# Moving batch 1's values and mixing steps into batch 0's output product, and the second channel weight's transfers ahead of them

## The chip, the cores and the metric

The kernel runs on one core of one Trainium2 chip. The metric is device time in microseconds (us) of one execution, as the median of several. Lower is better. The text calls the engines by the profile's names: PE is the matrix engine, DVE, ACT and POOL are the vector, scalar and GpSimd engines, and SP only issues transfers.

## The reference, cut to what matters

For each of 8 batches there are 8 heads of masked attention over 576 positions, and then an MLP mixer that works first across tokens and then across channels.

```
scores = scale * q @ k.T             # (8 batches, 8 heads, 576, 576), head_dim 64
masks: heads 0-3 see the last 32 positions; heads 4-7 every 4th of the last 128
attn = softmax(where(mask, scores, -1e9)) ; x = attn @ v   # as (batch, 576, 512)
xt = x.transpose(0, 2, 1)
h = maximum(xt @ w_tok1, 0) @ w_tok2          # 576 -> 256 -> 576, over tokens
u = x + h.transpose(0, 2, 1)
h2 = maximum(u @ w_ch1, 0) @ w_ch2            # 512 -> 1536 -> 512, over channels
out = u + h2
```

Inputs and output are float32; the kernel computes in float16 with float32 accumulation.

## The kernel before, in words

The work is one fully unrolled program. Every engine runs its instructions in the order in which the program writes them. For each batch there are these stages, named here by the tiles that the profile prints:

- **Loads and casts.** SP issues the float32 loads of q, k and v (tiles `l_q`, `l_k`, `lt` for the tails, `l_vn`, `l_vt`, `l_vd`, `l_vx`). POOL casts them to float16 (`c_q`, `c_k`, `c_t`, `vv`, `vt`; all of them at L102). A cast of q or k covers two heads, so it comes four times for each, numbered 0 to 3.
- **Turning q and k over.** PE transposes a cast tile into a PSUM bank, and ACT or DVE copies it out (L309 to L340 for batch 1; `bare_steps`, L363 to L391, for batch 2: one step `tails`, and q and k steps 0 to 3).
- **Scores.** PE multiplies, ACT takes the exponential out of PSUM (batch 1: L453 to L496, one pair of heads at a time). From batch 2 on `scores_twin` (L498) does two pairs of heads in one group of 24 matmuls at L510, which write six PSUM banks, then eight or so exponentials at L534, then masks on POOL.
- **Values.** Eight heads; PE into a bank (`av`, L592 to L617), and DVE divides by the row's sum into `xn`.
- **Token mixing.** h1: four steps of five matmuls (L619), with the relu on ACT. u: five steps, s = 4, 0, 1, 2, 3 in this order (L630); for batch 1 the sum with `xn` is taken by PE and copied out by ACT for s = 0 and 2, and by DVE for s = 4, 1, 3. Then u is transposed, four steps `emit_uT` (L656), each of which reads all of s = 0 to 3.
- **Channel products.** The first, `gp` (L768): 12 blocks of four 512-column matmuls with the weight `w3`, each evacuated with a relu into `gt`. The second, the output product `yp` (L801): 4 row blocks of two halves, each half 12 matmuls of 256 columns, with the weight `w4`; its first six matmuls use blocks 0 to 7 of `w4` at most, the next six use blocks 6 to 11. DVE adds u, and SP stores.

PSUM has eight banks, under three tags: `main` (3, for `gp` and `yp`), `sc` (2, for scores) and `fl` (3, for nearly everything else: transposes, values, h1, u, uT). A step that needs a bank of `fl` waits until an earlier user's copy out of a bank is done. The twin score group of batch 2 takes **all three** `fl` banks at once (L500 to L503): the first two for the scores of heads 0 and 1, the third for the small blocks and tails.

**The order around the change.** `interleave` (L827) writes the order by a planner's clock t in rough us. The main stream of a batch (its `gp`, then its `yp`) yields planned costs of 0.43 for half a `gp` block and 0.65 for a piece (six matmuls, half of a half) of `yp`. Every other step is a tuple (due time, cost, function); when its due time is at or below t, the step is written next, and t grows by its cost. While batch 0's two products run, the steps of batch 1's scores, values, mixing and uT, and the first of batch 2's, are written among them. Batch 1's `gp` starts when batch 0's `yp` is written out, and it needs all of batch 1's uT.

**Transfers of the weights.** `w3` (three parts) and `w4` (three parts, L999) are issued on POOL, so each issue stands in POOL's order among the casts. In the kernel before, the third part of `w3` is issued after the first two casts of batch 1, and the three parts of `w4` after the first twelve of them. Behind batch 1's last cast stands a `gate` (L867, L1006): a cast of one element from the first part of `w4` into batch 2's tail tile. SP can issue batch 2's loads only when that is done.

Of the kernel before, what the change touches and what calls it, by code (L numbers as in the profile page):

```python
# [68 lines left out]
def kernel(  # L69
# [181 lines left out]
    def cast_qk(b, nm, hp, eng):  # L251
        if (b, nm) not in c16:
            c16[(b, nm)] = sb.tile([128, 4, 4, 2, D], FP16, tag=f"c_{nm}", bufs=1, name=f"c_{nm}_{b}")
        copy(eng, c16[(b, nm)][:, hp],
             l32[(b, nm, hp // 2)][:, 2 * (hp % 2):2 * (hp % 2) + 2].rearrange("m h r d -> m r h d"))

    def cast_tails_qk(b, eng):
        c16[(b, "t")] = sb.tile([128, H, D], FP16, tag="c_t", bufs=1, name=f"c_t_{b}")
        copy(eng, c16[(b, "t")], l32[(b, "t")])

    def cast_tail_v(b, eng):
        copy(eng, vv[b % 2][0:64, 4, :, 0:64], l32[(b, "vt")])

    def cast_vn(b, s, eng):
        copy(eng, vv[b % 2][:, s, 0:4, 0:64], l32[(b, "vn")][:, s])

    def cast_vd(b, h, eng):
        copy(eng, vv[b % 2][:, 0:4, 4 + h:6 + h, 0:64],
             l32[(b, "vd")][:, h:h + 2].rearrange("m h r d -> m r h d"))

    def cast_vx(b, eng):
        copy(eng, vt[b % 2][:, :, 0:64], l32[(b, "vx")])

    def cast_steps(b, eng=nc.gpsimd):
        steps = [lambda: cast_tails_qk(b, eng)]
        for hp in range(4):
            for nm in ("q", "k"):
                steps.append(lambda nm=nm, hp=hp: cast_qk(b, nm, hp, eng))
        for s in range(4):
            steps.append(lambda s=s: cast_vn(b, s, nc.gpsimd))  # L280
        steps.append(lambda: cast_tail_v(b, nc.gpsimd))
        for h in (0, 2):
            steps.append(lambda h=h: cast_vd(b, h, nc.gpsimd))
        steps.append(lambda: cast_vx(b, nc.gpsimd))
        return steps
# [59 lines left out]
    def twinned(b):  # L345
        return b >= 2
# [81 lines left out]
    def veiled(b, hp):  # L428
        return b <= 1
# [249 lines left out]
    def turned(b):  # L679
        return b >= 2  # L680
# [18 lines left out]
    def score_steps(b, t0, dt, offs=(0.0, 0.7, 2.0), places=None, lag=0.0):  # L699

        steps = []
        if twinned(b):
            for g in range(2):
                f = scores_twin(b, g)
                at = t0 + g * dt
                steps.append((at, 0.86, lambda f=f: next(f)))
                for i in range(7 if g else 9):
                    steps.append((at + lag * (i + 1), 0.0, lambda f=f: next(f)))
            return steps
        for hp in range(4):  # L710
            at, at_s = places[hp] if places else (t0 + hp * dt, t0 + hp * dt + dt)
            for nm in ("q", "k"):
                steps.append((at + 0.9 * (nm == "k"), 0.28, lambda nm=nm, hp=hp: transposes(b, nm, hp)))
            g = (scores_plain if hp < 2 else scores_dil)(b, hp)
            for i in range(3):
                steps.append((at_s + offs[i], 0.42 if veiled(b, hp) else 0.21, lambda g=g: next(g)))
        return steps

    def value_steps(b, t0, dt):
        steps = []  # L720
        for h in range(H):
            def step(h=h):
                if h == 0:
                    xn[b] = sb.tile([128, 5, DM], FP16, tag="xn", bufs=2, name=f"xn_{b}")
                values(b, h)
            steps.append((t0 + dt * h, 0.29 if h < 4 else 0.18, step))
        return steps

    def mix_steps(b, t_h1, t_h1b, t_u, t_uT, du=1.0, turn=6.0, gap=2.6):
        h1 = [sb.tile([128, DM], FP16, tag="h1", bufs=4, name=f"h1_{b}_{jb}") for jb in range(2)]  # L730
        steps = []
        for half, at in ((0, t_h1), (1, t_h1b)):
            for jb in range(2):
                steps.append((at + 0.9 * jb, 0.55, lambda jb=jb, half=half: emit_h1(b, jb, half, h1[jb])))
        for i, s in enumerate((4, 0, 1, 2, 3)):
            steps.append((t_u + du * i, 0.44, lambda s=s: emit_u(b, s, h1)))
        if turned(b):
            for t, tail in ((2.0, True), (turn, False))[1 - b % 2:]:
                steps.append((t_u + t * du, 0.0, lambda tail=tail: uT_dma(b, tail)))
            for t, cb in ((0.0, 2), (0.0, 0), (gap, 3), (gap, 1)):  # L740
                steps.append((t_uT + t, 0.0, lambda cb=cb: uT_place(b, cb)))
        else:
            for i, cb in enumerate(CBS):
                steps.append((t_uT + 0.9 * i, 0.28, lambda cb=cb: emit_uT(b, cb)))
        return steps
# [155 lines left out]
    va = [st[2] for st in value_steps(0, 0.0, 1.0)]  # L901
# [90 lines left out]
    casts1 = cast_steps(1)  # L992
    for i in (0, 1):
        casts1[i]()
    load_w3(2)
    for i in (2, 4, 5, 7, 6, 8, 9, 10, 11):
        casts1[i]()
    for i in range(3):
        nc.gpsimd.dma_start(  # L999
            out=w4a[:, 4 * i:4 * i + 4],  # L1000
            in_=moe_w_ch2[512 * i:512 * i + 512, :].rearrange("(p i) c -> p i c", i=4))
    for cast in casts1[12:]:
        cast()

    new_qk(2)
# [8 lines left out]
    def at(t0, dt, fs):  # L1014
        return [(t0 + dt * i, 0.0, f) for i, f in enumerate(fs)]

    for b in range(B):
        steps = []
        if b == 0:
            steps += at(2.9, 0.0, [lambda: cast_qk(1, "q", 1, nc.scalar)])  # L1020
            steps += score_steps(1, 0, 0, (0.0, 0.7, 1.5),
                                 ((3.0, 4.9), (4.3, 6.6), (6.9, 9.2), (8.3, 11.0)))
            va = value_steps(1, 13.2, 0.7)
            steps += va[:4] + [(p + 0.3, c, f) for p, c, f in va[4:]]
            steps += mix_steps(1, 18.4, 20.8, 22.8, 31.4, 1.1)
            steps += at(24.0, 0.3, cast_steps(2))
            bare = bare_steps(2)
            scores2 = score_steps(2, 29.6, 4.4, lag=0.25)
            scores2 = sorted(scores2, key=lambda st: st[0])
            steps += [(t, 0.25, f) for t, f in zip((25.4, 26.4, 27.2, 28.0, 28.8, 34.8, 35.2, 35.6, 36.0), bare)]  # L1030
            steps += scores2[:10]
            steps += at(34.0, 0.0, [lambda: emit_loads_qk(3)])
        elif b == 1:
            va = value_steps(2, 0.0, 1.0)
            steps += [(0.8 + 0.4 * i, c, f) for i, (_, c, f) in enumerate(scores2[10:])]
            steps += [(t, c, f) for t, (_, c, f) in zip((2.2, 3.0, 4.8, 5.6, 8.2, 9.0, 10.4, 11.2), va)]
            steps += mix_steps(2, 7.0, 13.0, 15.1, 24.6, 1.0, 5.6, 0.8)
            casts = cast_steps(3)
            steps += [(6.0 + 0.5 * i, 0.0, casts[i]) for i in (0, 2, 4, 6, 8)]
            steps += [(9.5 + 1.0 * i, 0.0, lambda i=i: cast_qk(3, "q", i, nc.scalar)) for i in range(4)]  # L1040
            steps += score_steps(3, 21.0, 4.6, lag=0.1)
            steps += at(20.8, 0.9, load_steps(4))
            loads, turns, places = [], dma_steps(3), place_steps(3)

            def some_v(lo, hi):
                if not loads:
                    loads.extend(load_v_steps(3))
                for f in loads[lo:hi]:
                    f()

            steps += at(6.0, 0.0, [lambda: some_v(0, 4)]) + at(8.1, 0.0, [turns[0], turns[2], lambda: some_v(4, 7)])
            steps += at(10.6, 0.0, [turns[1], turns[4], lambda: some_v(7, 8)]) + at(12.6, 0.0, [turns[3]])
            steps += at(11.0, 0.3, casts[9:14]) + at(12.5, 0.0, places[0:3])
            steps += at(13.0, 0.3, casts[14:16]) + at(14.0, 0.0, places[3:]) + at(14.2, 0.0, casts[16:])
        else:
            late = 2.4 * (b % 2)
            if b + 1 < B:
                steps += value_steps(b + 1, 0.4, 0.95) + mix_steps(b + 1, 5.4 + late / 6, 9.0, 11.4, 22.4 + late)
            if b + 2 < B:
                steps += at(2.0, 0.6, cast_steps(b + 2)) + score_steps(b + 2, 16.6 + 1.25 * late, 4.5)  # L1060
                steps += at(8.5, 0.7, dma_steps(b + 2)) + at(12.0, 0.4, place_steps(b + 2))
            if b + 3 < B:
                steps += at(17.6, 0.9, load_steps(b + 3))
        interleave(gen_main(b), steps)
# [30 lines left out]
```

## Time and profile before

| | us |
|---|---|
| median of 3 runs | 286.30 (285.88 to 286.33) |
| the profiled execution | 286.22 |
| its span, first to last instruction | 284.4 |
| PE busy | 276.2 (97%) |
| ACT, DVE, POOL busy | 136.9, 130.7, 163.3 |
| batch 0's `gp` starts | 26.74 |
| batch 0's first `yp` matmul | 48.53 |
| batch 1's `gp` starts | 67.47 |

The profiled execution's own time is 1.8 us longer than its span. In a row of the timeline the columns are the start in us, the duration in us, the engine, the line, the operation, the tiles written and read, the shapes, and in brackets how long the engine stood idle before it and what ended that. A matmul's row lasts longer than its turn on PE, because matmuls overlap: matmuls of 512, 256 and 128 columns follow each other after 0.215, 0.110 and 0.056 us, while their rows are 0.38, 0.27 and 0.22 us long.

### The profile page before, as it was taken

To read this page: it belongs to the slowest core of one execution; us is meant where nothing else is said; L and a number is where in the kernel's file an instruction comes from. 1 tells how busy PE (TensorE), PEld (TensorE's weight loads), DVE (VectorE), ACT (ScalarE), POOL (GpSimd) and SP (SyncE) were. 2 spreads that over 40 slices of the span, in tenths; PEclk is the share of its full clock that TensorE was granted. 3 is DMA by queue.
4 is the path that set the end of the run, shared out by engine and by line. 5 is a ranking of instruction groups with operands and counts; after the bars stand their busy time and mean duration, and the time that the engine had idled before them with its cause. 6 is when DMAs were issued, how large, how long until landed. Compare 5 with 4: busy or idle time off the path is not lost.

```text
span 284.4 us, 7021 instructions
## 1 busy us (share of the span) xinstructions
PE 276.2 (97%) x2850; PEld 210.9 (74%) x2850; DVE 130.7 (46%) x275; ACT 136.9 (48%) x270; POOL 163.3 (57%) x220
## 2 busy tenths in 40 slices
PE   6899999999999999999999999999999999999995
PEld 2786677887676976697776976797767966896595
DVE  7776676356764155415640254426441274421022
ACT  2863765454454615383446625482546534225500
POOL 7980760587936998459961999179953930000000
PEclk9999999999999999999999999999999999999999
DMA  7999999984999999999979988299974210431023
GB/s 218 265 227 253 271 218 211 323 206 117 342 187 142 292 275 236 145 223 334 195 151 227 312 239 169 58 236 313 203 146 85 94 56 2 92 112 39 0 76 111
DMA packets 105695, 52.63 MB, mean 185 GB/s; under 512 B 73888, under 2 KB 104608, under 8 KB 105664
## 3 DMA queue, kind: packets, MB, share of 16 engines
q1 hardware_dynamic: 101424, 47.07, 69.2%
q0 software_dynamic: 2640, 3.94, 7.9%
q10 hardware_dynamic: 1600, 1.18, 1.4%
q8 instruction: 22, 0.36, 0.6%
q14 instruction: 9, 0.07, 0.1%
HBM read 37.07 MB, written 9.44 MB: 163 GB/s over the span
## 4 chain that ended last, share of the span: by engine, by line
PE 79%; DMA 7%; POOL 6%; SPq 2%; DVE 2%; issue 1%; ACT 1%; POOLq 0%; ACTq 0%
PE gp L768 25%; PE yp L801 25%; PE h1p L627 4%; PE gt L759 4%; PE up L639 4%; PE yp L818 3%; PE sc L510 2%; DMA l_k<-in_k_dram 2%; DMA w1p<-in_moe_w_tok_dram 2%; DMA kr<-c_k 2%; DMA l_q<-in_q_dram 2%; POOL c_q L102 1%; PE av L603 1%; PE av L608 1%; PE h1p L625 1%
## 5 line engine op out<-in xcount | busy, mean ns | idle before, releaser
L801 PE MATMUL yp<-w,gt 128*128 128x256 f16 x744 | 85.8, 273 | 0.0
L801 PEld LDWEIGHTS <-gt 128*128 128x128 f16 x744 | 76.1, 106 | 6.4
L106 ACT ACTIVATE gt<-gp 128x512 f16<-128x512 f32 x71 | 42.4, 597 | 73.5 <-PE gp L768 73.2
L768 PE MATMUL gp<-utd,w 128*128 128x512 f16 x144 | 54.7, 380 | 0.0
L768 PE MATMUL gp<-utm,w 128*128 128x512 f16 x144 | 54.6, 379 | 0.0
L768 PEld LDWEIGHTS <-w 128*128 128x128 f16 x384 | 38.9, 114 | 19.7 <-issue 0.5
L809 DVE TENSOR_TENSOR o<-yp,u 128x512 f32<-128x512 f32 x31 | 21.4, 692 | 63.4 <-PE yp L801 63.4
L112 POOL TENSOR_TENSOR attp<-attp,const 128x1280 f16<-128x1280 f16 x12 | 31.4, 2616 | 24.4 <-ACT attp L534 24.3
L112 DVE TENSOR_TENSOR xn<-av,rec 128x320 f16<-128x320 f32 x64 | 31.5, 492 | 2.2
L112 POOL TENSOR_TENSOR attd<-attd,const 128x1024 f16<-128x1024 f16 x12 | 25.4, 2134 | 1.9 <-ACT attd L534 1.9
L768 PE MATMUL gp<-uT,w 128*128 128x512 f16 x96 | 25.8, 380 | 0.0
L108 DVE TENSOR_SCALAR gt<-gp 128x512 f16<-128x512 f32 x25 | 17.2, 688 | 13.7 <-PE gp L768 13.0
L645 DVE TENSOR_TENSOR u<-up,xn 128x512 f16<-128x512 f32 x26 | 17.9, 690 | 6.2 <-PE up L639 6.2
L534 ACT ACTIVATE attp<-sc 128x480 f16<-128x480 f32 (+1 forms) x36 | 16.1, 536 | 7.3 <-PE sc L510 6.2
L102 POOL CAST c_k<-l_k 128x512 f16<-128x512 f32 x29 | 17.7, 622 | 2.1 <-DMA l_k<-in_k_dram 2.0
L102 POOL CAST c_q<-l_q 128x512 f16<-128x512 f32 x26 | 16.7, 648 | 2.5 <-DMA l_q<-in_q_dram 1.8
L106 ACT ACTIVATE h<-h1p 128x256 f16<-128x256 f32 x31 | 11.9, 384 | 11.9 <-PE h1p L627 11.5
L616 DVE RECIPROCAL rec<-av 128x5 f32<-128x5 f32 x64 | 12.2, 191 | 9.8 <-PE av L613 9.6
L399 POOL COPY kt<-kr 128x512 f16<-128x512 f16 x10 | 10.8, 1078 | 9.9 <-DMA kr<-c_k 7.7
L697 ACT COPY utd<-utm 128x512 f16<-128x512 f16 x12 | 12.7, 1117 | 5.8 <-DMA utm<-u 5.8
L102 POOL CAST vv<-l_vn 128x256 f16<-128x256 f32 x32 | 11.9, 413 | 4.0 <-DMA l_vn<-in_v_dram 4.0
L112 POOL TENSOR_TENSOR attt<-attt,const 128x512 f16<-128x512 f16 x12 | 13.9, 1162 | 0.0
(149 smaller groups left out, 465.2 us busy)
## 6 DMA issues: line engine op xcount, KB each, us to landing
out_dram<-o SPq DMA_DIRECT2D x71, 128.0 KB, 3.2
l_q<-in_q_dram SPq DMA_DIRECT2D x15, 512.0 KB, 6.7
l_k<-in_k_dram SPq DMA_DIRECT2D x14, 512.0 KB, 7.1
l_vn<-in_v_dram SPq DMA_DIRECT2D x32, 128.0 KB, 6.4
l_vd<-in_v_dram SPq DMA_DIRECT2D x16, 256.0 KB, 4.5
w<-in_moe_w_ch_dram POOLq DMA_DIRECT2D x6, 512.0 KB, 7.6
lt<-in_q_dram SPq DMA_DIRECT2D x8, 128.0 KB, 3.9
l_vt<-in_v_dram SPq DMA_DIRECT2D x8, 128.0 KB, 4.1
```

The lines of the kernel that those rows point to most:

```text
L102: eng.tensor_copy(out=out, in_=in_)
L106: nc.scalar.activation(out=out, in_=in_, func=AF.Relu)
L108: eng.tensor_scalar_max(out=out, in0=in_, scalar1=0.0)
L112: eng.tensor_tensor(out=out, in0=x, in1=y, op=ALU.mult)
L534: nc.scalar.activation(out=out, in_=in_, func=AF.Exp, scale=0.125)
L616: nc.vector.reciprocal(out=rec[:, :, 0], in_=av[:, :, 64])
L627: nc.tensor.matmul(out=p, lhsT=w[:, s, j], rhs=x[:, s, c], start=False, stop=(s == 3))
L645: nc.vector.tensor_tensor(out=u16(b, s), in0=blocks4(p), in1=blocks4(xn[b][:, s]), op=ALU.add)
L697: nc.scalar.copy(out=natural(uTd[:, cb - 2]), in_=uTm[i][:, cb].rearrange("p r m -> p m r"))
L768: nc.tensor.matmul(out=p, lhsT=w3_block(cb, mb), rhs=uT[(b, cb)][0], start=(i == 0), stop=(i == 3))
L801: nc.tensor.matmul(out=p[:, c], lhsT=gta[:, mb, a0:m0 + 512:4] if half else gta[:, mb, a0:a0 + 128], rhs=w4[mb][:, c], start=(mb == 0), st ...
L809: nc.vector.tensor_tensor(out=blocks4(o32), in0=blocks4(p), in1=u16(b, s), op=ALU.add)
```

## The change

The three issues of `w4` move from behind batch 1's twelfth cast to places among its casts: one after the casts of k 0 and 1, one after q 2 and 3, one after k 2 and 3. In batch 0's plan, batch 1's scores are spread a little wider; the values move from due time 13.2 to 20.4, the four h1 steps from 18.4 and 20.8 to 25.4 and 27.4, the u steps from 22.8 with a spacing of 1.1 to 28.8 with 0.95, and uT from 31.4 to 33.6. Batch 2's first casts, transposes and first score group move by 1 to 2.4. In batch 1's plan the score groups of batch 3 move by 0.5.

```diff
     load_w3(2)
-    for i in (2, 4, 5, 7, 6, 8, 9, 10, 11):
-        casts1[i]()
     for i in range(3):
+        for c in ((2, 4), (5, 7), (6, 8))[i]:
+            casts1[c]()
         nc.gpsimd.dma_start(
             out=w4a[:, 4 * i:4 * i + 4],
             in_=moe_w_ch2[512 * i:512 * i + 512, :].rearrange("(p i) c -> p i c", i=4))
-    for cast in casts1[12:]:
+    for cast in casts1[9:]:
         cast()
...
             steps += score_steps(1, 0, 0, (0.0, 0.7, 1.5),
-                                 ((3.0, 4.9), (4.3, 6.6), (6.9, 9.2), (8.3, 11.0)))
-            va = value_steps(1, 13.2, 0.7)
+                                 ((3.0, 5.2), (4.6, 7.2), (7.4, 10.0), (9.4, 12.2)))
+            va = value_steps(1, 20.4, 0.65)
             steps += va[:4] + [(p + 0.3, c, f) for p, c, f in va[4:]]
-            steps += mix_steps(1, 18.4, 20.8, 22.8, 31.4, 1.1)
-            steps += at(24.0, 0.3, cast_steps(2))
+            steps += mix_steps(1, 25.4, 27.4, 28.8, 33.6, 0.95)
+            steps += at(25.6, 0.3, cast_steps(2))
             bare = bare_steps(2)
-            scores2 = score_steps(2, 29.6, 4.4, lag=0.25)
+            scores2 = score_steps(2, 32.0, 4.4, lag=0.25)
             scores2 = sorted(scores2, key=lambda st: st[0])
-            steps += [(t, 0.25, f) for t, f in zip((25.4, 26.4, 27.2, 28.0, 28.8, 34.8, 35.2, 35.6, 36.0), bare)]
+            steps += [(t, 0.25, f) for t, f in zip((26.6, 27.6, 28.6, 29.8, 30.6, 35.2, 35.7, 36.2, 36.7), bare)]
...
-            steps += score_steps(3, 21.0, 4.6, lag=0.1)
+            steps += score_steps(3, 21.5, 4.6, lag=0.1)
```

## The prediction

> **What bounds the kernel now.** I read the cores' row first, then the busy times, and then went only to PE.
>
> ```profile
> core 0: 284.4 us, clock 0.998
> ```
> ```profile
> PE 276.2 (97%) x2850; PEld 210.9 (74%) x2850; DVE 130.7 (46%) x275; ACT 136.9 (48%) x270; POOL 163.3 (57%) x220
> ```
>
> PE is the bound, at full clock. The change adds and removes no matmul, so only PE's waits can move the time, and a wait removed or added in batch 0's stage goes to the end one to one: nothing behind it is idle enough to give it back. Next come PE's waits from batch 0's `gp` (26 us) to batch 1's (67.4 us), and the two of them that the waits view is too coarse for.
>
> ```profile
> PE sc L425 <- DVE kt L314: 0.5, 2, 0.4
> PE sc L510 <- DVE kt L385: 0.5, 1, 0.5
> ```
> ```profile
> 38.98 0.19 PE L423 MATMUL sm<-veil,const 128*128 128x64 f16 x1
> 39.01 0.19 PE L425 MATMUL sm<-qz,kt 128*128 128x64 f16 x1
> 39.28 0.22 PE L423 MATMUL sc<-veil,const 128*128 128x128 f16 x1
> ```
> ```profile
> 59.42 1.50 PE L801 MATMUL yp<-w,gt 128*128 128x256 f16 x12
> 60.88 0.27 PE L673 MATMUL tpu<-const,u 128*128 128x128 f16 x2
> ```
>
> The middle rows show how to read an idle time: matmuls follow each other every 0.03 us but last 0.19, so each idle figure hides about 0.16 us more. Three waits then cost 0.5 + 0.32 = 0.82 (batch 1's scores for k's copy) and 0.5 + 0.16 = 0.66 (batch 2's score group for the same). The fourth is 39.01 to 39.28, 0.24 (a bank of `sc`). The fifth: twelve `yp` matmuls at 0.110 end at 60.74, and uT starts at 60.88, so 0.14. Together 1.86 us: all that better placing could gain here.
>
> **Scores and first product.** I wrote the planner's order out by hand from the due times and costs; for the kernel before it gives the sequence of the trace. In the new order one half of `gp` more stands between each k transpose and its score, but DVE's chain of copies in front is as long as before and `gp` block 5's relu joins it. I leave 0.28 of the 1.06 (0.82 + 0.24) there; bounds 0 and 1.06. Gone: 0.78. Batch 2's score group now stands behind u steps, its k copy is done earlier, and uT stands elsewhere: 0.66 + 0.14 gone. Total gone **1.58**.
>
> **When `yp` starts.** Ahead of the first `yp` the new order has eight values and two h1 steps fewer.
>
> ```profile
> 48.53 0.82 PE L801 MATMUL yp<-w,gt 128*128 128x256 f16 x6
> 49.18 0.27 PE L625 MATMUL h1p<-xn,w1t 128*128 128x256 f16 x1
> 49.29 0.60 PE L627 MATMUL h1p<-xn,w1p 128*128 128x256 f16 x4
> 49.73 0.27 PE L625 MATMUL h1p<-xn,w1t 128*128 128x256 f16 x1
> ```
>
> An h1 step is 0.55 (49.18 to 49.73), a piece of `yp` (six matmuls, half of a half) 0.65 (48.53 to 49.18); values at the planner's costs are 4 x 0.29 + 4 x 0.18 = 1.88. First `yp`: 48.53 - 1.88 - 1.10 - 0.78 = **44.8**; the third part of `w4` is needed after eight more matmuls, at 45.7.
>
> **The transfers.** The next rows are POOL's timeline; then the two queues' shares of the 16 DMA engines in three stretches, 32.5 to 35, 35 to 41 and 41 to 49 us (q0 is POOL's, q1 SP's); then the landing times of `w4`'s parts.
>
> ```profile
> 33.49 1.18 POOL L102 CAST c_k<-l_k 128x512 f16<-128x512 f32 x2 [0.35 <-DMA l_k<-in_k_dram]
> ...
> 38.08 1.62 POOL L999 DMA_DIRECT2D w<-in_moe_w_ch_dram  x3
> ...
> 41.71 0.41 POOL L102 CAST vt<-l_vx 128x256 f16<-128x256 f32 x1
> 43.67 0.18 POOL L867 CAST lt<-w 1x1 f32<-1x1 f16 x1 [1.55 <-DMA w<-in_moe_w_ch_dram]
> 50.88 0.62 POOL L102 CAST c_t<-lt 128x512 f16<-128x512 f32 x1 [7.03 <-DMA lt<-in_k_dram]
> 52.16 0.61 POOL L102 CAST c_q<-l_q 128x512 f16<-128x512 f32 x1 [0.67 <-DMA l_q<-in_q_dram]
> 53.67 0.62 POOL L102 CAST c_k<-l_k 128x512 f16<-128x512 f32 x1 [0.90 <-DMA l_k<-in_k_dram]
> ```
> ```profile
> q0 software_dynamic: 383, 0.39, 93.5%
> q1 hardware_dynamic: 447, 0.12, 29.3%
> ```
> ```profile
> q1 hardware_dynamic: 2419, 0.99, 71.9%
> q0 software_dynamic: 164, 0.31, 34.4%
> ```
> ```profile
> q0 software_dynamic: 380, 1.36, 86.1%
> ```
> ```profile
> DMA to landing us min/median/max: 5.5/7.4/10.4
> ```
>
> An issue costs POOL 1.62 / 3 = 0.54 us. The three of them now delay casts of q and k 2 and 3 by 0.54 and 1.08, which the wider scores cover, and the last is issued at about 35.8. The DMA engines are full from 32 on, so an earlier issue only changes who goes first. From 35 on, q0 (rest of `w3`, all of `w4`) needs 34.4% of 6 + 86.1% of 8 = 8.95 us, and q1 (batch 1's v) 71.9% of 6 = 4.3: together 13.3, at the 1.0 to 1.2 that full stretches reach done at 46 to 48.3; I take 47.3. In the first stretch the queues took turns packet by packet (383 to 447), so POOL's long packets took three quarters of the time. On that share `w4` runs ahead (8.95 / 0.93 from 35, 44.6; landing about 1 later, **45.6**, just in time for 45.7) and v ends last, its landing, final cast and the gate (0.2 + 0.41 + 0.18) at **48.1** instead of 43.85. Batch 2's loads start 4.3 later.
>
> [...] Service in order of issue instead would be the late-weight rival below.
>
> From the gate's end to the end of batch 2's tail cast took 51.50 - 43.85 = 7.65, to the first k cast 54.29 - 43.85 = 10.44, with `w4`'s end still in the way; I take 0.7 off each for that, an estimate: 55.1 and 57.8. On PE the values start five pieces after 44.8, at 48.1; batch 2's tails follow after the values, five more pieces and two h1 steps, 1.88 + 5 x 0.65 + 1.10, at 54.35, and wait 0.75; the first k transposes follow 2.2 later (0.22, 0.65, 0.55, 0.22, 0.55), at 57.3, and wait 0.5. Sum with 0.1 for `w4`: **1.35**, bounds 0 (gate at 46.5 or before) and 3 (gate at 48.6, nothing taken off).
>
> **The u chain.** What copies banks out, on ACT and then DVE (49 to 67 us), and the end of the small exponentials:
>
> ```profile
> L383 ACT COPY qt<-tp_q 128x512 f16<-128x512 f16 x4 | 2.4, 590 | 2.2 <-PE tp_q L378 2.2
> L643 ACT CAST u<-up 128x512 f16<-128x512 f32 x2 | 1.2, 588 | 2.0 <-PE up L639 2.0
> ```
> ```profile
> L102 DVE COPY uT<-tpu 128x640 f16<-128x640 f16 x3 | 1.8, 599 | 1.7 <-PE tpu L667 1.3 <-PE tpu L675 0.4
> L385 DVE COPY kt<-tp_k 128x512 f16<-128x512 f16 x2 | 1.4, 692 | 1.8 <-PE tp_k L378 1.8
> L645 DVE TENSOR_TENSOR u<-up,xn 128x512 f16<-128x512 f32 x2 | 1.4, 680 | 0.0
> L387 DVE COPY kr<-tp_k 128x512 f16<-128x512 f16 x2 | 0.8, 420 | 0.2 <-PE tp_k L378 0.2
> ```
> ```profile
> 60.43 0.40 ACT L534 ACTIVATE attt<-sc 128x256 f16<-128x256 f32 x1
> 60.69 1.53 ACT L534 ACTIVATE attp<-sc 128x480 f16<-128x480 f32 x3
> ```
>
> The new order from there is: u 4, u 0, q 1, k 1, u 1, a piece of `yp`, u 2, the score group, two exponentials, **u 3**, four exponentials, uT 2, a piece, uT 0, a piece, q 2, uT 3, k 2, q 3, uT 1, k 3, two pieces, batch 1's `gp`. Three `fl` banks serve all but `yp`:
>
> - u 1 wants u 0's bank: u 0's 0.59 copy on ACT, behind only q 1 and k 1 (0.44 of PE) and the matmul's tail of 0.16: about **0.3** (0 to 0.4). Whether u 4 also waits for ACT (up to 0.4) I take as hidden under k's wait above.
> - the score group's third `fl` bank is u 2's: its copy ends 0.16 + 0.59 behind u 2, the group reaches that bank after some 0.4: **0.4**.
> - u 3 comes when the group holds all three `fl` banks. Before, uT was in this place with twelve `yp` matmuls ahead, and still waited: it started 0.05 behind the exponential that ends at 60.83, 1.46 after the group's end (59.42). No `yp` lies between now: **1.45**, and it delays all behind it.
> - uT 2 reads u 3, and only exponentials, which PE does not run, lie between: 0.16 + 0.68 for DVE's sum, less the three transposes of s = 0 to 2: **0.75**.
> - q 3, uT 1 and k 3 each follow two short PE steps behind the bank that they want, whose copies take 0.59, 0.6 and 0.42 plus k's second copy of about 0.3; PE has 0.5 to cover each: **0.8** (0.4 to 1.1).
>
> Sum 3.7. With the transfers 5.05, less 1.58: 3.5 slower. The profiled execution, 0.08 under the median of its runs, goes from 286.22 to **289.7**.
>
> **The rivals.**
>
> *Late weight, 291.4.* If the DMA engines serve in order of issue, v goes first and `w4`'s last part lands near 48.4: `yp` waits 2.7 at 45.7, while the gate comes early and batch 2's casts cost nothing; u 4's 0.4 shows. 286.2 - 1.6 + 2.7 + 0.4 + 3.7. For it: `w4`'s landings of 5.5 to 10.4 us after issue; against it: the packet counts above.
>
> *Filled waits, 285.1, faster.* If PE's queue is not in written order but lets the four pieces of `yp` that remain pass u 3 and what hangs on it, 4 x 0.65 = 2.6 of the 3.7 are hidden; with transfers on time 286.2 - 1.6 + 1.1 = 285.7, and with u 1's and the score group's waits filled by the piece before them, 285.1. It turns to the slower side once the transfers cost over 1.1. Against it: at 60.88 PE waited for a bank with `yp` next in order, and `yp` did not pass.
>
> *Only u 3 waits, 286.2, no change.* Transfers on time and all other banks free in time: 286.2 - 1.6 + 1.45. It needs my five smaller waits to be wrong together.
>
> **How the numbers follow.** Forecast 0.70; late weight 0.13; filled waits 0.09; only u 3, 0.08. The forecast's own range is 287.6 (transfers free, small waits at their low ends) to 291.4 (transfers 3). Leaving out the no-change and faster cases (0.17) and little above, the range is 287.2 to 291.7. A measurement here can tell about 0.2%, 0.57 us, from no change: faster 0.09, same 0.08, slower 0.83.
>
> **What would show it.** PE's waits should have a row of u at L639 for an exponential at L534, over 1 us; one of uT for DVE's u at L645; batch 2's transposes for POOL's casts. The rows of k's copy at L314 should shrink below 0.3 and that at L385 go. The first `yp` starts near 44.8 and batch 1's `gp` near 71.0 (67.47 before); the gate stands near 48. Wrong: the gate before 46 with `yp` waiting for a weight (late weight); `yp` running between the score group and u 3 (filled); or `gp` of batch 1 at 67 or earlier.

## The result and the profile after

The changed kernel takes 290.6 us (median of 4 runs, 289.26 to 291.51) against 286.14 for the kernel before it (4 runs, 285.88 to 286.33): a ratio of 1.0149 [1.0127, 1.0171], slower by 4.5 us. The forecast was 289.7, worked out for the profiled execution. That execution is the longest of the four, 291.51 with a span of 289.7; against the profiled execution before (286.22, span 284.4) it has lost 5.29.

First the cores' row and the busy times.

```profile
core 0: 289.7 us, clock 0.994
```
```profile
PE 279.2 (96%) x2850; PEld 212.4 (73%) x2850; DVE 131.0 (45%) x275; ACT 136.6 (47%) x270; POOL 162.9 (56%) x220
```

The number of matmuls is the same, 2850, and yet PE is busy 3.0 us longer. A busy time that grows at a constant count can mean that single matmuls became longer, a first hint that waiting is not the whole loss. It is no proof, because the 0.16 us that each new wait hides in the row ahead of it counts as busy too. The second hint is the clock, 0.994 instead of 0.998.

PE's waits, all of those in batch 0's stage. In each row: what waits, for what, us in total, how often, the longest.

```profile
PE up L639 <- ACT attt L534: 1.4, 1, 1.4
PE tpu L673 <- DVE u L645: 0.6, 1, 0.6
PE tp_k L378 <- POOL c_k L102: 0.5, 1, 0.5
PE tp_q L309 <- POOL c_q L102: 0.4, 1, 0.4
...
PE sc L425 <- DVE kt L314: 0.2, 1, 0.2
PE tp_k L378 <- DVE u16t L654: 0.2, 1, 0.2
PE tp_k L309 <- POOL c_k L102: 0.2, 1, 0.2
PE tp_q L378 <- ACT qt L383: 0.2, 1, 0.2
...
PE sc L510 <- ACT u L643: 0.2, 1, 0.2
```

The row of k's copy at L385 is gone, the one at L314 has shrunk, and eight rows have come: five on the mixing chain and among the transposes, and three for casts on POOL. The next rows are PE's timeline from the end of batch 2's score group to batch 1's first `gp`.

```profile
63.08 0.24 PE L510 MATMUL sc<-tt,kt 64*128 64x64 f16 x4
64.69 0.38 PE L639 MATMUL up<-h,w 128*128 128x256 f16 x2 [1.37 <-ACT attt L534]
...
65.16 0.33 PE L673 MATMUL tpu<-const,u 128*128 128x128 f16 x3
66.08 0.29 PE L673 MATMUL tpu<-const,u 128*128 128x128 f16 x1 [0.59 <-DVE u L645]
66.16 0.31 PE L675 MATMUL tpu<-const,u16t 128*128 128x128 f16 x1
66.26 1.49 PE L801 MATMUL yp<-w,gt 128*128 128x256 f16 x6
67.54 0.63 PE L664 MATMUL tpu<-const,u 128*128 128x128 f16 x4
...
68.08 1.49 PE L801 MATMUL yp<-w,gt 128*128 128x256 f16 x6
69.36 0.44 PE L378 MATMUL tp_q<-const,c_q 128*128 128x128 f16 x4
...
73.06 1.03 PE L768 MATMUL gp<-uT,w 128*128 128x512 f16 x4
```

Two things are to be read here. u 3 and uT 2's last transpose wait 1.37 and 0.59 of shown idle time, 1.53 and 0.75 with the 0.16 that each figure hides. And behind them six output-product matmuls take 66.26 to 67.54, 0.213 each instead of 0.110; the second six take the same. The windows of that stretch show why. After the stretch: busy time of PE (with its instructions), PEld, DVE, ACT and POOL, then the granted clock, the share of the transfer engines, and GB/s.

```profile
62.00:64.00 2.00, 1.17 (x27) 0.83 (x25) 0.51 (x1) 1.16 (x4) 2.00 (x5) 1.00 0.93 221
64.00:66.00 2.00, 0.79 (x7) 0.54 (x6) 0.67 (x1) 1.57 (x5) 1.92 (x6) 1.00 1.11 342
66.00:68.00 2.00, 1.92 (x13) 1.55 (x14) 0.02 (x1) 1.49 (x3) 1.96 (x3) 0.51 0.77 255
68.00:69.40 1.40, 1.40 (x10) 1.03 (x9) 0.49 (x1) 0.14 (x1) 1.40 (x1) 0.50 0.81 156
69.40:72.00 2.60, 2.19 (x30) 1.83 (x29) 1.88 (x5) 1.17 (x2) 2.60 (x3) 0.99 0.90 301
```

The clock is granted in full until 66, at half from 66 to 69.4, and in full again. Twelve matmuls lose 12 x (0.213 - 0.110) = 1.24; uT 0, five transposes, takes 67.54 to 68.08, 0.54 instead of five turns of 0.056: 0.26 more. The half clock costs 1.5 us in this execution.

The transfers: POOL's timeline, then the two queues (q0 is POOL's, q1 SP's) between 35 and 41 us, and the weight's last issue there with its time to landing.

```profile
35.94 0.53 POOL L999 DMA_DIRECT2D w<-in_moe_w_ch_dram  x1
...
40.60 0.40 POOL L102 CAST vv<-l_vn 128x256 f16<-128x256 f32 x1 [3.39 <-DMA l_vn<-in_v_dram]
46.74 0.40 POOL L102 CAST vv<-l_vn 128x256 f16<-128x256 f32 x1 [5.74 <-DMA l_vn<-in_v_dram]
...
49.89 0.18 POOL L867 CAST lt<-w 1x1 f32<-1x1 f16 x1
54.44 0.61 POOL L102 CAST c_t<-lt 128x512 f16<-128x512 f32 x1 [4.38 <-DMA lt<-in_k_dram]
...
57.50 0.61 POOL L102 CAST c_k<-l_k 128x512 f16<-128x512 f32 x1 [1.14 <-DMA l_k<-in_k_dram]
```
```profile
q0 software_dynamic: 449, 1.07, 91.9%
q1 hardware_dynamic: 789, 0.20, 20.3%
```
```profile
w<-in_moe_w_ch_dram POOLq DMA_DIRECT2D x1, 512.0 KB, 10.4
```

Before, q1 had 71.9% of the 16 engines in this stretch and moved 0.99 MB; now it has 20.3% and moves 0.20. The weight took the transfer engines from v: v's last casts, and the gate behind them, stand at 49.89 instead of 43.67. The weight's third part, issued at 35.94, lands 10.4 later, at 46.3. Over the six us POOL's queue had 91.9% of the engines, where the forecast took 0.93. The prediction read turns packet by packet from 383 against 447. Here the six us as a whole give 449 against 789, uneven from 35 to 37 us (235 against 580); from 37 to 44 us the queues moved 372 and 367 packets, 1.35 and 0.09 MB, with 95.8% and 10.3% of the engines: nearly packet for packet, and the queue with the long packets had most of the time.

### The profile page after: what moved, and what is told of

It reads as the page before. It is cut to its first block, busy times and chain, and to the rows that moved or that the text cites. A ratio compares the mean times of both kernels' runs of the same rounds, so it can differ in the third digit from the quotient of the medians.

```text
span 289.7 us, 7022 instructions
## 1 busy us (share of the span) xinstructions
PE 279.2 (96%) x2850; PEld 212.4 (73%) x2850; DVE 131.0 (45%) x275; ACT 136.6 (47%) x270; POOL 162.9 (56%) x220
## 4 chain that ended last, share of the span: by engine, by line
PE 81%; DMA 11%; POOL 2%; SPq 2%; DVE 1%; ACT 1%; issue 1%; POOLq 0%; ACTq 0%
PE yp L801 26%; PE gp L768 25%; DMA l_k<-in_k_dram 5%; DMA l_vd<-in_v_dram 5%; PE h1p L627 4%; PE up L639 4%; PE gt L759 4%; PE yp L818 4%; PE sc L510 3%; DMA l_q<-in_q_dram 1%; PE av L603 1%; PE av L608 1%; PE h1p L625 1%; PE up L650 1%; PE av L601 1%; SPq L207 1%
## 5 line engine op out<-in xcount | busy, mean ns | idle before, releaser
L801 PE MATMUL yp<-w,gt 128*128 128x256 f16 x744 | 86.8, 275 | 0.0
L112 POOL TENSOR_TENSOR attp<-attp,const 128x1280 f16<-128x1280 f16 x12 | 31.4, 2615 | 28.5 <-ACT attp L534 28.5
L768 PE MATMUL gp<-uT,w 128*128 128x512 f16 x96 | 24.8, 379 | 0.0
L616 DVE RECIPROCAL rec<-av 128x5 f32<-128x5 f32 x64 | 12.2, 190 | 10.5 <-PE av L613 10.3
```

Of the source, the lines that this page charges most:

```text
L112: eng.tensor_tensor(out=out, in0=x, in1=y, op=ALU.mult)
L616: nc.vector.reciprocal(out=rec[:, :, 0], in_=av[:, :, 64])
L768: nc.tensor.matmul(out=p, lhsT=w3_block(cb, mb), rhs=uT[(b, cb)][0], start=(i == 0), stop=(i == 3))
L801: nc.tensor.matmul(out=p[:, c], lhsT=gta[:, mb, a0:m0 + 512:4] if half else gta[:, mb, a0:a0 + 128], rhs=w4[mb][:, c], start=(mb == 0), st ...
```

## The experiments

All compare with runs of the kernel before on the same chip and in the same job (medians of 286.3 to 286.8 us). The changed kernel was not run again there, so a kernel made from it is best held against the changed kernel's ratio, 1.0149 [1.0127, 1.0171].

**One part of the change alone.** First the weight's issues, with the plan of before.

```diff
     for i in range(3):
+        for c in ((2, 4), (5, 7), (6, 8))[i]:
+            casts1[c]()
         nc.gpsimd.dma_start(
```

> The plan of the kernel before, with the three issues of w4 moved among batch 1's casts alone. Theory (w4's long packets starve batch 1's v, so the gate and batch 2's loads come late): the gate stands near 49 instead of 43.85, batch 2's tail cast ends near 55 where PE wants it at 53.8, the k cast 2 us late; about 288 us (287.3 to 289), slower by 0.4 to 1%. Rival (only the placement of the steps costs, an earlier issue is free): 286.1, no change.

Measured 294.42 (293.4 to 294.94), ratio 1.0259 [1.0219, 1.0300]. Its waits of PE:

```profile
PE av L603 <- POOL vv L102: 4.7, 1, 4.7
PE av L613 <- POOL vv L102: 0.8, 1, 0.8
PE sc L425 <- DVE kt L314: 0.5, 2, 0.4
...
```

This is above the range given. v comes late, as expected, but the wait is at another place: the values wait 5.5 us for v, which the expectation had not counted, and batch 2's casts, which it had, cost PE nothing in this view. Behind the wait stands a clock of 0.50 in the windows from 48 to 52 us. The kernel before's waits for k's copies are still there. Then the plan alone, with the weight issued at its old place:

```diff
-            va = value_steps(1, 13.2, 0.7)
+            va = value_steps(1, 20.4, 0.65)
...
-            steps += mix_steps(1, 18.4, 20.8, 22.8, 31.4, 1.1)
+            steps += mix_steps(1, 25.4, 27.4, 28.8, 33.6, 0.95)
```

> The changed plan, with w4 issued where it was before. Theory: yp starts near 45 and its third part of w4 lands near 49.5, so PE waits about 3 us there; the gate stays near 44 and batch 2's casts cost nothing; u 3 still waits 1.5 and uT 0.75 after it; about 291 us (290 to 292.5). Rival (the issue's place does not matter): no wait of yp for a weight, 289 us.

Measured 294.57 (293.04 to 297.04), ratio 1.0284 [1.0215, 1.0354].

```profile
PE yp L801 <- DMA w<-in_moe_w_ch_dram: 3.8, 2, 2.5
PE up L639 <- ACT attt L534: 1.4, 1, 1.4
PE tpu L673 <- DVE u L645: 0.6, 1, 0.6
...
```

This too is above the range given. The output product, which comes earlier, waits 3.8 for the weight (about 3 was expected), and the four runs have mean clocks of 0.981 to 0.994. So the halves of the change need each other: each alone costs 8 us, together 4.5. The waits of u 3 and uT, the same in size here as in the changed kernel, belong to the plan.

**The bank behind u 3's wait.** u 3 is put ahead of the score group, nothing else.

```diff
-            steps.append((t_u + du * i, 0.44, ...))
+            steps.append((t_u + du * i - (0.93 if b == 1 and s == 3 else 0.0), 0.44, ...))
```

> The changed kernel with u 3 alone put ahead of the score group. Theory (what is short is banks: the group holds all three of fl): the wait of 1.5 for the exponential passes to uT, which now stands behind the group; only uT's wait of 0.75 for u 3 goes; 289.4 us (288.8 to 290). Rival (u 3's place is the fault): both go, 2.3 us and more, 287.5 us or less.

Measured 288.88 (288.55 to 288.95), ratio 1.0075 [1.0046, 1.0104].

```profile
PE tpu L673 <- ACT attt L534: 1.4, 1, 1.4
...
```

The median is inside the range given, and the rival's 287.5 or less is out. The wait is passed on: whatever step comes next behind the group, now uT 2, waits those 1.4 for the exponentials that hold the banks. uT's wait for the data of u 3 is gone, since u 3 is done long before; and with one wait instead of two the clock stays up (0.999 or more in all four runs). Next, uT is moved behind two pieces of the output product as well.

```diff
-            steps += mix_steps(1, 25.4, 27.4, 28.8, 33.6, 0.95)
+            steps += mix_steps(1, 25.4, 27.4, 28.8, 34.5, 0.95)
```

> As the kernel with u 3 ahead of the score group, and uT's four steps 0.9 later in the plan, so that two pieces of yp (1.31 us) stand between the group and the next user of an fl bank. Theory: the wait for the exponential shrinks to about 0.2, uT's for u 3 goes, and PE no longer idles 2 us in 3, so the clock stays up; 287.3 us (286.7 to 288). Rival (the waits of the other engines only move on): not under 289 us.

Measured 288.54 (287.51 to 291.23, 10 runs), ratio 1.0084 [1.0055, 1.0113]: above the range given, and no better than the kernel with u 3 alone moved.

```profile
PE tp_k L378 <- DVE uT L102: 0.6, 1, 0.6
...
```

The 1.4 is gone, but uT and the steps q 2 to k 3 are now crowded into less of the output product, and a new wait for a bank has come between them, with smaller ones beside it.

**Is the half clock from idling?** Six matmuls that compute nothing are put into u 3's wait.

```diff
-            steps += scores2[:10]
+            steps += scores2[:10] + [(32.55, 0.0, lambda: warm(6))]
```

> The changed kernel with six 512-column matmuls on an idle tile written between batch 2's score group and u 3; they compute nothing that is used (6 x 0.215 = 1.29 us, less than the 1.53 us for which u 3 waits). Nothing else is moved, so every wait keeps its place and its size. Theory (two near stops of PE, 1.4 and 0.6 us within 3 us, are what halves the granted clock for the next 3.3 us): the twelve output-product matmuls behind uT run at 0.110 instead of 0.213 us, the granted clock in 66 to 69.4 us is above 0.95, and the median is 289.3 (288.8 to 289.8) with no run at 291. Rival (the clock falls for another reason than idling, for instance a budget spent by then): clock still 0.5 there, median 290.6 as the changed kernel, or more by what the extra matmuls take.

Measured 290.2 (288.65 to 291.34, 6 runs), ratio 1.0119 [1.0088, 1.0149]. The first of the windows that had half the clock (the next, to 70, has 1.00 too):

```profile
66.00:68.00 2.00, 1.99 (x25) 1.86 (x25) 0.49 (x1) 1.63 (x3) 1.88 (x4) 1.00 0.72 243
```

The clock theory holds: with PE kept going the clock is full in all six runs (1.000), while two of the changed kernel's four had 0.994. The rest of the expectation misses. The median is above the range given, its ratio cannot be told from the changed kernel's, and runs up to 291.3 remain at full clock, so the half clock is not the whole spread between runs. And a wait stands in this profile that the changed kernel's did not show:

```profile
44.92 1.04 PE L801 MATMUL yp<-w,gt 128*128 128x256 f16 x8
46.63 1.14 PE L801 MATMUL yp<-w,gt 128*128 128x256 f16 x9 [0.67 <-DMA w<-in_moe_w_ch_dram]
```

Here batch 1's first casts came early, the first `yp` starts at 44.92, and after eight matmuls it waits for the weight's third part, 0.67 + 0.16 = 0.83. In the changed kernel's profile the first of them came 0.8 later (28.74 instead of 27.95), PE waited for those, and the weight was in time. One of the two waits hides the other: the first of the eight values starts at 49.03 here and at 48.96 in the changed kernel's profile.

**The gate.** Batch 2's loads of q and k are written ahead of v's casts.

```diff
-    for cast in casts1[9:]:
-        cast()
     new_qk(2)
     gate(l32[(2, "t")][0:1, 0, 0:1], w4[0][0:1, 0:1])
...
+    for cast in casts1[9:]:
+        cast()
     load_v(2)
```

> The changed kernel with the gate and batch 2's q and k loads written ahead of batch 1's last casts (those of v) instead of behind them; the plan is untouched. Theory (batch 2's transposes wait because SP cannot issue batch 2's loads before v's last cast, while the transfer engines pause at 49 to 52 us): the gate stands near 41 to 43.5 us instead of 49.9, the waits of k's transposes and of the tails for POOL's casts (0.69 + 0.13) are gone, PE's u 3 and uT waits and the fall of the clock stay: median 289.8 (289.2 to 290.3). Rival (the q and k loads take transfer time from v, and the values, which start at 49, wait for it): v's last cast later than 49.5, the values wait, and the median is 290.6 to 292.

Measured 290.15 (289.3 to 291.61), ratio 1.0128 [1.0104, 1.0152].

```profile
...
PE yp L801 <- DMA w<-in_moe_w_ch_dram: 0.7, 1, 0.7
...
```

The gate now stands at 41.31, and the wait for c_k is gone, as expected. The weight's 0.7 is in this profile instead. The 0.13 ahead of the tails was no wait for c_t: that cast now ends at 53.11, and the tails' transposes still start 0.12 after PE is free, at 55.31. The median is inside the range given, but the difference from the changed kernel is smaller than either's spread, so no gain in time is shown. The clock falls here too, to 0.50 from 66 to 68 us.

**All three together** (u 3 earlier, uT later, the gate earlier).

> The changed kernel with three edits: u 3 ahead of the score group, uT due 0.9 later (two pieces of the output product between the group and uT), and the gate with batch 2's q and k loads ahead of v's casts. Theory (the waits are those of banks and of casts, each cured on its own): 288.5 (measured with the first two) less 0.6 to 0.8 for the casts' waits: 287.8 (287.2 to 288.3), still slower than the kernel before by about 1.5 us, since the short steps of q 2 to k 3 among uT still follow one another too closely for three banks. Rival (the q and k loads delay v): 288.5 or more.

Measured 287.8 (287.4 to 288.13), ratio 1.0036 [1.0022, 1.0049]: as expected, and still not the kernel before.

```profile
PE tp_k L378 <- DVE uT L102: 0.6, 1, 0.6
PE yp L801 <- DMA w<-in_moe_w_ch_dram: 0.3, 1, 0.3
...
```

**The weight's third part, and a respaced plan.** In the first row block of the output product the two first pieces go ahead of the two second ones, so that the third part is needed 0.65 later. The first edit had a fault: a `yield` too many in the loop made the planner count three of each row block's four pieces twice, in all batches, so that every step beside the output products came too early.

```diff
+                for part in range(4):
+                    half, lo = (part % 2, part // 2) if first else (part // 2, part % 2)
...
+                    if part < 3:
+                        yield 0.65
...
                     yield 0.65
```

> The kernel of the filled wait (six extra 512-column matmuls between the score group and u 3) with one more edit: in the first row block of batch 0's output product the two first pieces (weight blocks 0 to 5 of either half) come before the two second pieces (blocks 6 to 11), the halves in two banks, so that the weight's third part is needed 0.65 us later. Theory (the third part lands at 46.6 whatever PE does and its lateness, 0.83 us in the profiled execution of the filled kernel, is what varies from run to run, since the clock no longer does): the wait in the output product shrinks to 0.2 or less, the median is 289.6 (289.2 to 290.0), and the range of the runs is under 1.5 us instead of 2.7. Rival (another cause of the spread): the median comes down by no more than 0.3 and runs above 291 remain.

The second kernel has this beside all three earlier edits, and a plan respaced by the copies:

```diff
-        eng = nc.scalar if cb == 2 else nc.vector
+        eng = nc.scalar if cb == (1 if b else 2) else nc.vector
...
-            steps += mix_steps(1, 25.4, 27.4, 28.8, 34.5, 0.95)
+            mix = mix_steps(1, 25.4, 27.4, 28.8, 33.6, 0.95)
+            dues = (28.8, 29.75, 31.05, 31.65, 32.0, 34.6, 34.9, 35.9, 37.0)
+            steps += mix[:4] + [(t, c, f) for t, (_, c, f) in zip(dues, mix[4:])]
...
-            steps += [(0.8 + 0.4 * i, c, f) for i, (_, c, f) in enumerate(scores2[10:])]
+            steps += [(0.3, 0.25, bare[8])]
+            steps += [(1.6 + 0.4 * i, c, f) for i, (_, c, f) in enumerate(scores2[10:])]
```

> The kernel with all three earlier edits (u 3 ahead of the score group, uT later, the gate and batch 2's q and k loads ahead of v's casts), the output product's first pieces reordered as in the run beside it, and the short steps respaced by the copies that free their banks: a piece of the output product between q 1 and k 1, uT 2 copied by DVE and uT 1 by ACT, uT 2 and 0 after two pieces, then a piece, uT 3, q 2, a piece, uT 1, k 2, q 3, and k 3 only in batch 1's first product. Theory (what was left there are copies that follow one another on one engine, 2.3 us in all, and the weight's 0.5): 286.3 (285.7 to 287.0), level with the kernel before or just under it. Rival (DVE's copies are simply too many for four pieces): 287.5 or more, with waits on DVE's copies moved and not gone.

Measured 299.33 (298.66 to 300.15), ratio 1.0446 [1.0418, 1.0473], and 296.9 (296.45 to 298.7), ratio 1.0370 [1.0337, 1.0402]. They say nothing on their questions; what they show is only that the plan's due times are worth 9 to 10 us where they slip in all batches. The same two with the two added lines ahead of the last `yield` taken out, and in the second with two of batch 2's values put ahead of its second score group:

> The reordered first row block again, now with each piece counted once by the planner (in the two runs before this, three of each row block's four pieces had been counted twice, in every batch's plan, so that all steps beside the output products came too early). The filled wait is in it as before. Theory (the weight's third part lands at 46.2 to 46.6 whatever PE does, and how late that is varies from run to run): the wait in the output product is 0.2 or less, the values come 0.6 earlier and may wait up to 0.4 for v; median 289.7 (289.3 to 290.2), range of the runs under 1.5 us. Rival (another cause of the spread): a median within 0.3 of the filled kernel's 290.2 and runs above 291.

Measured 289.45 (288.63 to 290.9), ratio 1.0100 [1.0069, 1.0131]. The weight's wait is gone from the profile and the median is in the range given, but the runs spread by 2.3 us, so the weight is not the spread, or not all of it. The kernel before spread by 2.1 us in the same job (17 runs, 286.06 to 288.17).

> The respaced kernel again with each piece counted once, and with two of batch 2's values ahead of its second score group. Theory (copies that follow one another on one engine, 2.3 us in the combined kernel, and the weight's 0.5, are what keeps it above the kernel before): 286.3 (285.8 to 287.0) beside a kernel before of 286.5. Rival (DVE's copies are too many for four pieces): 287.5 or more, with waits on copies moved and not gone.

Measured 287.99 (287.71 to 288.93, 12 runs), ratio 1.0041 [1.0024, 1.0058]: the rival's side.

```profile
PE sc L510 <- DVE xn L112: 0.7, 1, 0.7
PE h1p L625 <- DVE xn L112: 0.4, 1, 0.4
...
```

The rows for waits between uT 2 and k 3 are gone, and others of the same kind stand one stage later, in batch 1's `gp`, where k 3 and the second score group were pushed. Moved, and not gone.

**The kernel before without its own waits.** The transfers stay as they were; the scores are spread as in the change, a piece of the output product goes between the last k transposes and the score group, and uT and q 2 to k 3 are spaced by pieces. The first row block is reordered as above.

```diff
-                                 ((3.0, 4.9), (4.3, 6.6), (6.9, 9.2), (8.3, 11.0)))
-            va = value_steps(1, 13.2, 0.7)
+                                 ((3.0, 5.2), (4.6, 7.2), (7.4, 10.0), (9.4, 12.2)))
+            va = value_steps(1, 13.7, 0.7)
...
-            steps += mix_steps(1, 18.4, 20.8, 22.8, 31.4, 1.1)
+            mix = mix_steps(1, 18.4, 20.8, 22.8, 31.4, 1.1)
+            steps += mix[:9] + [(t, c, f) for t, (_, c, f) in zip((32.0, 32.8, 33.9, 34.7), mix[9:])]
...
-            scores2 = score_steps(2, 29.6, 4.4, lag=0.25)
+            scores2 = score_steps(2, 30.2, 4.4, lag=0.25)
...
-            ... (25.4, 26.4, 27.2, 28.0, 28.8, 34.8, 35.2, 35.6, 36.0), bare)]
+            ... (25.4, 26.4, 27.2, 28.0, 28.8, 35.7, 36.0, 36.9, 37.1), bare)]
```

> The kernel before, with its transfers as they were and only its own waits taken away: batch 1's scores spread as in the changed kernel (values 0.5 later in the plan), one piece of the output product between the last k transposes and batch 2's score group, uT and the steps q 2 to k 3 spaced by pieces, and the first row block's two first pieces ahead of its second ones, so that the weight's third part, which lands at 49.5, is needed 0.65 later. Theory (the spread scores are worth 0.78 and the group's k copy 0.4 to 0.66 by themselves; neither needs the values, mixing and weight issues moved): gone 1.2 to 1.4, less up to 0.2 of waiting for the weight: 1.0 to 1.4 under the kernel before of the same job, ratio 0.995 to 0.9965. Rival (the weight's landing holds the output product where it was, so that the scores' gain is lost in a wait for it): a wait for the weight of 0.5 or more and a ratio of 0.998 to 1.0.

Measured 284.93 (284.25 to 285.72) against 286.73 for the kernel before in the same job, ratio 0.9942 [0.9918, 0.9965]: 1.8 less, somewhat more than the 1.0 to 1.4 expected. This beats both kernels. What each of the edits gives by itself was not measured. Its waits view shows no wait of PE between 26 and 80 us. Its cores' row and the start of batch 1's `gp`, which was at 67.47 before and 73.06 in the changed kernel:

```profile
core 0: 282.5 us, clock 1.000
```
```profile
65.80 1.03 PE L768 MATMUL gp<-uT,w 128*128 128x512 f16 x4
```

Batch 0's `gp` starts at 26.64 here, so the stage to batch 1's `gp` takes 39.16 us instead of 40.73: 1.57 of the 1.86 that the prediction named as all that better placing could gain.

## Why the prediction was right, step by step

The direction was right, and so was the mechanism in the main: the waits of the u chain and of k's casts came at the instructions named. Two of the waits forecast, those of the tails and of u 1, did not come, and two losses of the profiled execution were not in the sum, the half clock and batch 1's late first casts. Where a step is measured here, it is an idle time of the profile after plus the hidden 0.16, or a distance between rows.

| step | forecast | measured |
|---|---|---|
| k copies, score bank, uT's bank of before | -1.58 | -1.5: the five waits of 1.86 are gone, and the scores keep 0.34 |
| first `yp` | 44.8 | 45.68, and 44.92 where batch 1's casts were on time |
| `w4`'s third part | lands 45.6, costs 0.1 | lands 46.3, costs 0; 0.83 in the filled kernel and in the one with the gate moved |
| gate; batch 2's first k cast, their ends | 48.1; 57.8 | 50.07; 58.11 |
| batch 2's casts | 1.25 (tails 0.75, k 0.5) | 0.69 (k alone) |
| u 1 behind u 0 | 0.3 | none; k 1 beside it 0.36, for u 4's bank |
| score group's third bank | 0.4 | 0.31 |
| u 3 | 1.45 | 1.53 |
| uT 2 for u 3 | 0.75 | 0.75 |
| q 3, uT 1, k 3 | 0.8 | 0.89 |
| half clock | not in the sum | 1.5 |
| batch 1's first casts | not in the sum | 0.88 (0.36 and 0.20 idle, each with 0.16) |
| batch 1's `gp` starts | 71.0 | 73.06 |

The rows behind two of these readings, batch 1's first casts and u 4's bank:

```profile
30.69 0.40 PE L309 MATMUL tp_q<-const,c_q 128*128 128x128 f16 x4 [0.36 <-POOL c_q L102]
32.20 0.40 PE L309 MATMUL tp_k<-const,c_k 128*128 128x128 f16 x4 [0.20 <-POOL c_k L102]
...
60.08 0.38 PE L378 MATMUL tp_k<-const,c_k 128*128 128x128 f16 x4 [0.20 <-DVE u16t L654]
```

The measured rows add up to -1.5 + 0.69 + 0.36 + 0.31 + 1.53 + 0.75 + 0.89 + 1.5 + 0.88 = 5.4. From batch 0's `gp` to batch 1's the changed kernel took 46.21 us (26.85 to 73.06) instead of 40.73 (26.74 to 67.47), 5.48 more, so the rows account for the stage. The two profiled executions differ by 5.29: the stage began 0.11 later, and 0.3 came back behind it, so that "one to one" was nearly but not quite right.

**Right as a mechanism.** That the group takes all three banks, and that u 3 then waits for exponentials with nothing between, was the largest term; the kernel with u 3 moved shows it, since the same 1.4 moves to the next step in line. Without the wait of data in uT the clock's fall goes too, and the two together bring the ratio from 1.0149 to 1.0075.

**Mis-sized.** The first term is that of the transfers. The gate came 2.0 later than forecast, yet the first k cast ended only 8.0 behind it (10.4 before, 9.7 in the forecast). Its loads had the transfer engines to themselves: between 49 and 57 us POOL's queue moved nothing, while before, between 43.8 and 54 us, it held 39.9% of the engines with the end of `w4`. So the two casts ended nearly when forecast (tails 55.05 against 55.1, k 58.11 against 57.8), and k's wait was 0.69 instead of 0.5. The tails' 0.75 did not come, because PE itself was free for them only at 55.17, 0.8 later than forecast, by then behind the casts' end. The second term is the weight's third part. It came 0.7 later than forecast, and the price of 0.1 was too low by as much: the filled kernel and the one with the gate moved, whose first casts were early, both paid 0.83. In the changed kernel's own profile it cost nothing by luck, because late casts had held PE up by 0.88 already.

**Missing.** The half clock was no term of the sum. The profile before did not show it (cut into windows of 2 us, its clock is 1.00 in all of them up to 282 us); the changed kernel's does, 0.51 from 66 to 68 us, behind the two waits that the sum had as 1.45 and 0.75, next to each other in a stretch with little matrix work. The late casts' 0.88 was not in the sum either. It does not look like a part of the change: nothing ahead of these casts in the program's order differs between the kernels. Over the fourteen profiled executions the first of them starts between 27.05 and 29.10, at 28.74 in this one, and five of the kernels made from the changed one have 27.78 to 27.95. What makes it vary is not shown.

**Luck in the number.** The sum was meant for the profiled execution, and that came out at 291.51, 1.8 above it. The median is nearer because two of the four runs kept the clock, about which the sum said nothing. The two runs at full clock, 289.26 and 290.04, lie on both sides of the forecast; the two with a clock of 0.994, 291.15 and 291.51, are 1.7 above them on average, about what the half clock costs.

**The rivals.** The late weight was not the 2.7 of its rival, but it is there: 0 to 0.83 in the profiled executions with the change's transfers and plan, and 3.8 where the weight stays at its old place. The filled waits are out: no `yp` matmul passed u 3 in the order of PE's rows (u 3 at 64.69, the next `yp` at 66.26). "Only u 3 waits" is out as well, since five smaller terms stand beside it; its own sum comes to 286.05 and not 286.2, which is no change either.

**What stays open.** The runs of the filled kernel spread from 288.65 to 291.34 at full clock, and those of the reordered one from 288.63 to 290.9. Late casts and the late weight do not explain it in the filled kernel, because either leads to nearly the same start of the values (48.96 in the changed kernel's profile, 49.03 in the filled kernel's). Much of it may not belong to the change at all, since the kernel before spread by up to 2.1 us in one job. No profile of a run above 291 at full clock was taken, so its cause is not known.

## What to carry to other kernels

List, for each pool of buffers that short steps share, who holds the last ones and what releases them: a step that takes all of them needs independent work behind it until a bank is free again (u 3 waited 1.53 us for that), and moving one waiting step can hand its wait to the next, as it did here (1.4 us, from u 3 to uT 2). Before moving a chain of dependent steps to make room for another, look at what the waits themselves need: here a few due times and one reordered row block, with the transfers left alone, gave 0.6%, while the large move cost 1.5%. And where a transfer is issued earlier into full queues, ask whose transfer it delays (here v's, whose fourth part was cast at 46.74 instead of 39.68), and put that delay on the same line of the sum.

## What the runs showed of the hardware that was not expected

**Two short waits brought half the clock.** From 63.2 to 66.3 us PE ran four matmuls of u 3 and five transposes, with idle times of 1.37 and 0.59, and was then granted half its clock for 3.4 us. It does not come in every run: two of the changed kernel's four and two of the six with the gate moved have a mean clock of 0.994 or less. With six useless matmuls in the first wait, none of the twelve runs of the filled and the reordered kernel has less than 0.998. (In the reordered kernel's faulty first form, where other waits stand beside, two of six do, at 0.993 and 0.992.) A single idle time of 1.37, in the kernel with u 3 moved, had no such effect in its four runs. How long two waits must be, and how near each other, is not shown.

**The weight's queue took the time of v's.** With the weight issued among the casts, SP's queue fell from 71.9% to 20.3% of the transfer engines between 35 and 41 us. The fourth part of v was cast at 46.74 in the changed kernel (39.68 before), and in the kernel with the issues alone the values waited 5.5 us for v. The weight's packets were the longer ones (449 for 1.07 MB against 789 for 0.20), but no run changes the length of the packets alone, so that it is the length that decides is not shown.
